# A causal mask moved to GpSimd, four turns moved to TensorE, and new instruction orders in a fused attention and FFN kernel

## The chip, the cores and the metric

The kernel runs on one core of one Trainium2 chip. A core has five engines that run side by side, each through its own list of instructions in order: TensorE (PE in the profile, with its weight loads as PEld), VectorE (DVE), ScalarE (ACT), GpSimd (POOL) and SyncE (SP), which here only issues DMA transfers. An instruction waits until those that it depends on are done, and everything behind it on the same engine waits with it. The metric is the device time of one execution in microseconds.

## The reference

Eight batches of eight heads, 576 positions, 64 channels a head. Attention with a forgetting gate `f`, then a gated FFN with a convolution of three taps over the positions:

```python
scores = scale * np.matmul(q, k.transpose(0, 1, 3, 2))
cum = np.cumsum(np.log(np.clip(f, 0.0001, 1.0)), axis=-1)
decay = cum[:, :, :, None] - cum[:, :, None, :]
scores = np.where(causal, -1000000000.0, scores + decay)
attn = softmax(scores)                       # over the keys
x = np.matmul(attn, v)                       # heads side by side: (8, 576, 512)
h = np.maximum(x @ w_in, 0.0)                # 512 -> 1024
conv_out[s] = cw[0]*h[s-1] + cw[1]*h[s] + cw[2]*h[s+1]
out = (h * sigmoid(conv_out)) @ w_out        # 1024 -> 512
```

The inputs and the output are float32; the kernel computes in 16-bit types with float32 sums.

## The kernel before

The work is cut into 16 half batches `hb` of four heads. Each has two head pairs `i = 2*hb + p`, and two half batches make one batch `b` of the FFN. Every step is a named task of a `Plan`, and the string `ORDER` lists all tasks by hand; `plan.play` calls them in that sequence. As an engine runs its own instructions in order, `ORDER` fixes each engine's list, the SyncE queue included. A suffix `@ACT`, `@DVE` or `@POOL` chooses the engine where a task allows several. Tasks take rooms of small rings: four PSUM tiles `ps`, six `pp` tiles for exponentials, two scratch tiles `pd`, three output tiles `ob`, five `ht`, four `u`.

The tasks, with the lines of their instructions:

- `ld0`, `ld1`, `tp`, `cl`: for half batches 0 and 1, q and k are loaded plainly (L208), turned by TensorE (L215) and copied out of PSUM (L221 on ScalarE, L223 on VectorE). From half batch 2 on, `q{hb}.0` and `q{hb}.1` load and turn q and k in one DMA transpose (L229). Half batches 2 to 7 are clamped by VectorE (L235), and `rw` adds the rows of the decay (L251, L252); from 8 on, `fi` fills these rows by two DMAs instead (L243 from a block of zeros named blank, L245).
- `dca`, `dcl`, `dcs`, `dck`, `ki`: the gate's clip, logarithm, running sum and rows. The gate is loaded twice, into both halves of a tile (L271, L272).
- `sd`, `st`, `so`: scores of the diagonal blocks, the tail and the blocks below the diagonal (L359). `ed`, `et`, `eo`: their exponentials (L400, L379, L417) on ScalarE.
- The causal mask, for the diagonal blocks and the tail only. For half batches in `MASK_PE` TensorE adds a mask into PSUM ahead of the scores (L367), and the exponential goes straight to its 16-bit tile. For the others the exponential goes to a float32 scratch tile, and GpSimd selects from it (`md` at L403, `mt` at L382).
- `v`, `va`: v is loaded (L258) and cast (L266, L268). `pv`: the product with v (L441, L445). `n`: division by the row sum on VectorE (L453, L455).
- Turning x for the FFN: `t` on TensorE (L462, L464) and a copy `tx` (L472); or, for half batches in `XD`, one DMA transpose on SyncE (L467).
- The FFN of batch `b`, in eight blocks `ff`: `f` is the first product (L481), `r` the relu on ScalarE (L491), `c` and `d` the convolution on VectorE (L496, L498), `a` tanh on ScalarE (L501), `g` the gate on VectorE (L505), `o` the second product (L516), `k` copies of the last 64 columns (L510), `e` evacuations (L522, L526) and `s` stores (L532, L537, L540). For the last batch `o7.c.ff` is issued block by block for five chunks `c` of rows.
- `wi`, `wo` load the weights by parts (L551), `wic`, `woc` cast them (L559).

Before, the two choices are:

```python
MASK_PE = (0, 1, 2, 3, 4, 5, 6, 7)
XD = (10, 11, 12, 13, 14, 15)
```

Of the kernel before, what the change touches and what calls it, by code (L numbers as in the profile page):

```python
# [17 lines left out]
ld0 ld0.1.1 ld0.0.0 ld0.0.1 ld0.1.0 tp0.0.0 tp0.0.1 ld1 dca dcl tp0.1.0 tp0.1.1 cl0.0.0@ACT dcs dck ki@POOL ld1.0.0  # L18
cl0.1.0@DVE cl0.1.1@ACT v0.0 cw cl0.0.1@DVE ld1.0.1 tp1.0.0 q2.1 q2.0 v0.2 tp1.0.1 cl1.0.0@ACT cwt cl1.0.1@DVE sd1
tp1.1.0 cl1.1.0@ACT so1.0 eo1.0 v0.3 ed1 tp1.1.1 v0.1 va1.0@POOL cl1.1.1@DVE sd0 so0.0 cl2.0 rw1 so1.1 eo0.0 so0.1  # L20
eo1.1 ed0 v0.4 va1.1@POOL eo0.1 sd2 va0.0@ACT cl2.1 rw2 st0 sd3 so3.0 ed2 wi1 et0 so3.1 eo3.0 so2.1 eo3.1 pv0.0 q3.1
ed3 va0.1@DVE pv0.1 eo2.1 so2.0 eo2.0 wi0 n0.0 st1 et1 cl3.1 wic1@ACT pv1.0 q3.0 pv1.1 wic0@POOL wi3 wic3@POOL q5.0
n1.0 sd4 wi2 wic2@POOL n1.1 t1 q5.1 n0.1 t0 tx0@DVE sd5 tx1@DVE so4.1 ed5 ed4 cl5.0 f0.0 r0.0 st2 eo4.1 f0.1 v1.0 f0.2
r0.1 et2 v1.2 r0.2 so5.0 c0.0 so4.0 eo4.0 cl3.0 d0.0 so5.1 c0.1 d0.1 eo5.1 h0 f0.3 f0.4 rw3 a0.0 r0.3 v1.1 f0.5 cl5.1
f0.6 r0.4 c0.2 g0.0 d0.2 c0.3 v1.3 rw5 eo5.0 a0.1 g0.1 va2.0@DVE wo2 c0.4 sd7 r0.6 c0.6 st3 et3 ed7 sd6 ed6 q4.1 r0.5
so7.1 eo7.1 so6.0 so7.0 eo7.0 eo6.0 d0.4 v1.4 d0.3 d0.6 cl4.1 wo1 va2.1@POOL q4.0 so6.1 st5 eo6.1 pv2.0 sd11 a0.3
va3.0@ACT va3.1@POOL n2.0 c0.5 pv2.1 et5 sd10 wo0 woc0@POOL n2.1 q6.1 t2 g0.3 pv3.0 a0.6 ed11 ed10 pv3.1 q6.0 d0.5
a0.4 tx2@DVE n3.0 a0.2 n3.1 v2.0 f0.7 r0.7 woc2@ACT a0.5 cl4.0 so11.0 woc1@POOL t3 so10.0 so11.1 tx3@DVE v2.3 f1.0
eo11.1 c0.7 d0.7 eo10.0 eo11.0 g0.5 g0.4 g0.6 f1.1 f1.2 r1.0 g0.2 rw4 wo3 f1.3 a0.7 r1.1 so10.1 f1.4 cl6.0 v2.2 v2.4
r1.2 sd8 g0.7 eo10.1 st4 c1.0 r1.4 cl6.1 r1.3 c1.3 d1.3 c1.4 et4 sd9 v2.1 ed8 rw6 so9.0 ed9 d1.0 so9.1 q7.1 f1.5  # L30
woc3@POOL va4.0@DVE o0.0 d1.4 eo9.1 so8.1 eo9.0 q9.0 c1.2 h1 a1.0 q7.0 a1.3 eo8.1 so8.0 v3.0 eo8.0 o0.1 e0.0@ACT c1.1
va5.0@POOL va4.1@ACT sd13 v3.2 g1.0 r1.5 zc v3.1 so13.1 d1.2 eo13.1 k0@DVE f1.6 ed13 pv5.0 g1.3 pv4.0 r1.6 d1.1 n5.0
pv4.1 sd12 n4.0 n4.1 a1.4 va5.1@DVE so12.1 a1.2 g1.2 f1.7 cl7.1 pv5.1 ed12 a1.1 t4 r1.7 c1.7 n5.1 o0.2 v3.3 cl7.0 d1.7
g1.1 tx4@ACT rw7 t5 s0.0 eo12.1 tx5@ACT g1.4 a1.7 c1.6 va7.0@POOL o0.3 so12.0 eo12.0 q9.1 v4.0 so13.0 e0.1@DVE f2.0
v3.4 st6 v4.3 va6.0@POOL sd15 eo13.0 d1.6 et6 f2.1 sd14 c1.5 r2.0 d1.5 c2.0 ed15 r2.1 a1.6 so15.0 g1.7 f2.2 g1.6 d2.0
c2.1 a1.5 ed14 fi9 g1.5 r2.2 f2.3 so14.0 r2.3 f2.4 pv6.0 c2.3 eo14.0 eo15.0 r2.4 n6.0 so14.1 q8.1 so15.1 d2.3 c2.4
o1.0 st9 d2.1 d2.4 eo14.1 eo15.1 st7 h2 a2.0 pv7.0 et7 k1@POOL a2.1 sd19 g2.0 s0.1 et9 a2.3 q8.0 o1.1 va6.1@ACT pv6.1
n7.0 c2.2 q10.0 ed19 e1.0@ACT va7.1@POOL n6.1 fi8 so19.1 eo19.1 f2.5 r2.5 t6 g2.3 f2.6 sd18 tx6@ACT so18.0 r2.6 d2.2
g2.1 c2.5 pv7.1 md19 c2.6 f2.7 q10.1 n7.1 ed18 md18 so19.0 a2.4 g2.4 eo18.0 o1.4 st8 d2.6 eo19.0 d2.5 r2.7 sd16 a2.6
# [67 lines left out]
def kernel(  # L107
# [11 lines left out]
    nc = tc.nc  # L119
# [191 lines left out]
    def decay_log():  # L311
        nc.scalar.activation(fsb, fsb, AF.Ln)
        nc.scalar.preload_act_table(AF.Exp)
# [422 lines left out]
```

## Time and profile before

| what | value |
|---|---|
| median of three runs | 255.22 us (253.63 to 257.57) |
| profiled execution | 254.81 us, of it a span of 253.1 us between first and last instruction |
| granted TensorE clock, mean | 0.985 |
| busy: TensorE, VectorE, ScalarE, GpSimd | 230.6, 215.3, 209.3, 60.2 us |
| DMA | 49.98 MB, mean 197 GB/s |

The page of the profile lists busy time by engine, the span in 40 equal slices (a digit is the busy share in tenths), the chain of work that ended last, and the costliest groups of instructions with their mean duration and the idle time of the engine in front of them, with what ended it. Matmuls are pipelined and their ends are modelled, so a busy TensorE is not one at its peak.

### The profile page before, as it was taken

The page shows a single profiled execution, that of the slowest core. Times are in us where ns is not written, and L with a number is a line of the kernel's source. Part 1 is how long each engine was busy: PE and PEld are TensorE (multiplying, and loading weights), DVE is VectorE, ACT ScalarE, POOL GpSimd, SP SyncE. Part 2 cuts the span into 40 slices and gives each one's busy share as a digit, 9 for nine tenths or more (in the row PEclk, how much of TensorE's full clock was granted, in tenths as well). Part 3 has the DMA queues.
Part 4 walks back from the last instruction along what each step waited for, and adds up shares of the span by engine and source line. Part 5 has one row for each costly group of instructions (what it writes and reads, how often), then busy time and mean ns, then how long its engine had stood idle before and what let it go on. Part 6 is the DMA issues. An engine that isn't in the chain of part 4 may idle for free.

```text
span 253.1 us, 6392 instructions
## 1 busy us (share of the span) xinstructions
PE 230.6 (91%) x2618; PEld 146.2 (58%) x2618; DVE 215.3 (85%) x322; ACT 209.3 (83%) x285; POOL 60.2 (24%) x92
## 2 busy tenths in 40 slices
PE   0799989688999999999999999999959999999992
PEld 0687765357555766766565665665645755644440
DVE  5756064999999999999999989999949999999970
ACT  2746948799899989999899999999957999679661
POOL 8302011101407102221731145402414150000100
PEclk9979999999999999999999999999989999999999
DMA  7993999999999989999999999999998954045046
GB/s 161 326 276 76 218 223 168 233 220 243 223 247 209 218 187 222 237 233 222 194 245 206 242 194 255 213 185 275 230 179 174 198 163 88 7 128 201 6 166 208
DMA packets 121013, 49.98 MB, mean 197 GB/s; under 512 B 111010, under 2 KB 111010, under 8 KB 120984
## 3 DMA queue, kind: packets, MB, share of 16 engines
q1 hardware_dynamic: 120434, 48.41, 88.9%
q0 software_dynamic: 304, 0.73, 0.9%
q10 hardware_dynamic: 246, 0.44, 0.6%
q8 instruction: 20, 0.33, 0.5%
q14 instruction: 9, 0.07, 0.1%
HBM read 21.11 MB, written 10.17 MB: 124 GB/s over the span
## 4 chain that ended last, share of the span: by engine, by line
PE 57%; DVE 15%; DMA 13%; ACT 6%; issue 4%; SPq 2%; POOL 0%; ACTq 0%; DVEq 0%
PE ps L516 21%; PE ps L481 15%; PE ps L359 9%; PE ps L441 6%; DMA qk<-in_q_dram 5%; DVE u L496 4%; DVE u L498 3%; ACT pp L417 3%; DMA qk<-blank 3%; DVE hg L505 2%; DMA qk<-in_k_dram 2%; DMA u<-in_f_dram 2%; PE ps L445 2%; DVE xm L455 1%; PE ps L367 1%
## 5 line engine op out<-in xcount | busy, mean ns | idle before, releaser
L481 PE MATMUL ps<-xt,w_in_f 128*128 128x512 f16 (+1 forms) x512 | 69.3, 286 | 2.1 <-POOL w_in_f L559 1.6
L359 PE MATMUL ps<-qk 128*128 128x64 bf16 (+2 forms) x576 | 63.9, 242 | 4.5 <-DMA qk<-blank 2.6
L417 ACT ACTIVATE pp<-ps 128x1024 f16<-128x1024 f32 x64 | 64.0, 1042 | 2.8 <-PE ps L364 1.9
L516 PE MATMUL ps<-w_out_f,hg 128*128 128x512 f16 x256 | 59.3, 379 | 0.0
L498 DVE SCALAR_TENSOR_TENSOR u<-ht,cwt,u 128x576 f32<-128x576 f16 x64 | 56.2, 895 | 0.7
L496 DVE SCALAR_TENSOR_TENSOR u<-ht,cwt 128x576 f32<-128x576 f16 x64 | 54.0, 853 | 0.8 <-ACT ht L491 0.7
L501 ACT ACTIVATE hg<-u,cw 128x576 f16<-128x576 f32 x64 | 48.8, 788 | 5.5 <-DVE u L498 5.2
L359 PEld LDWEIGHTS <-qk 128*128 128x128 bf16 x576 | 39.8, 99 | 22.9 <-issue 4.6
L481 PEld LDWEIGHTS <-w_in_f 128*128 128x128 f16 x512 | 34.3, 98 | 31.3 <-POOL w_in_f L559 1.9
L505 DVE SCALAR_TENSOR_TENSOR hg<-hg,ht 128x576 f16<-128x576 f16 x64 | 50.2, 810 | 0.5 <-ACT hg L501 0.5
L491 ACT ACTIVATE ht<-ps 128x576 f16<-128x576 f32 x64 | 41.6, 674 | 6.3 <-DVE hg L505 2.6
L516 PEld LDWEIGHTS <-hg 128*128 128x128 f16 x256 | 23.8, 98 | 25.8 <-DVE hg L505 0.8
L403 POOL TENSOR_SCALAR_AFFINE_SELECT pp<-pd 128x1024 f16<-128x1024 f32 x16 | 20.4, 1282 | 55.8 <-ACT pd L400 55.8
L441 PE MATMUL ps<-va,pp 128*128 128x65 f16 x640 | 25.0, 196 | 1.4 <-ACT pp L417 1.2
L455 DVE TENSOR_TENSOR xm<-ps,rc 128x896 f16<-128x896 f32 (+1 forms) x32 | 24.2, 758 | 1.1
L441 PEld LDWEIGHTS <-pp 128*128 128x128 f16 x640 | 23.0, 99 | 3.7 <-ACT pp L417 1.1
L400 ACT ACTIVATE pd<-ps 128x1024 f32<-128x1024 f32 x16 | 16.4, 1041 | 5.0 <-PE ps L359 4.2
L400 ACT ACTIVATE pp<-ps 128x1024 f16<-128x1024 f32 x16 | 16.1, 1040 | 4.1 <-PE ps L359 4.1
L510 POOL COPY tl<-hg 128x512 f16<-128x512 f16 (+1 forms) x9 | 5.9, 669 | 45.6 <-DVE hg L505 45.6
L453 DVE RECIPROCAL rc<-ps 128x14 f32<-128x14 f32 (+1 forms) x32 | 6.6, 206 | 11.5 <-PE ps L441 7.7
L367 PE MATMUL ps<-mask,ident 128*128 128x512 bf16 (+1 forms) x40 | 14.7, 370 | 0.7 <-ACT pp L417 0.6
L266 POOL CAST va<-vf 128x1024 f16<-128x1024 f32 x7 | 8.5, 1226 | 25.9 <-PE ps L359 11.6
(91 smaller groups left out, 202.8 us busy)
## 6 DMA issues: line engine op xcount, KB each, us to landing
vf<-in_v_dram SPq DMA_DIRECT2D x32, 256.0 KB, 4.3
out_dram<-ob SPq DMA_DIRECT2D x14, 512.0 KB, 2.8
qk<-blank SPq DMA_DIRECT2D x8, 540.0 KB
ob<-in_moe_w_in_dram SPq DMA_DIRECT2D x4, 512.0 KB
ob<-in_moe_w_out_dram SPq DMA_DIRECT2D x4, 512.0 KB, 4.6
vf<-in_v_dram SPq DMA_DIRECT2D x8, 128.0 KB, 2.9
out_dram<-ob SPq DMA_DIRECT2D x4, 256.0 KB
out_dram<-ob SPq DMA_DIRECT2D x7, 128.0 KB, 2.8
```

Source lines behind the costliest of these rows:

```text
L359: nc.tensor.matmul(o, tk[:, h * S + k0:h * S + k0 + 128], tq[:, h * S + q0:h * S + q0 + n], start=first, stop=last and not by_matmul(hb, h))
L400: nc.scalar.activation(o, ps_of(f"sd{i}").rearrange("p (s c) -> p s c", s=2), AF.Exp, scale=SCALE)
L417: nc.scalar.activation(pair(i)[:, s, 512:1536], ps_of(f"so{i}.{s}"), AF.Exp, scale=SCALE)
L441: nc.tensor.matmul(ps[:, c:c + D + 1], block(hb, h, m, n), va[:, h, m, 0:D + 1], start=(m == 0), stop=(m == n))
L455: nc.vector.tensor_tensor(x.rearrange("p (j h d) -> p j h d", j=a, d=D), got[:, :, :, 0:D], r.unsqueeze(3).broadcast_to((128, a, g, D)), o ...
L481: nc.tensor.matmul(ps[:, c:c + n], w_in_f16[:, cc, 128 * ff:128 * (ff + 1)], xt[:, cc // 2, x:x + n], start=(cc == 0), stop=(cc == NCC - 1))
L491: nc.scalar.activation(ht_of(b, ff)[:, 1:1 + S], ps_of(f"f{b}.{ff}")[:, 0:S], AF.Relu, scale=0.5)
L496: nc.vector.scalar_tensor_tensor(u, ht[:, 0:S], cwt[:, ff, 0:1], ht[:, 1:1 + S], op0=ALU.mult, op1=ALU.add)
L498: nc.vector.scalar_tensor_tensor(u, ht[:, 2:2 + S], cwt[:, ff, 1:2], u, op0=ALU.mult, op1=ALU.add)
L501: nc.scalar.activation(hg_of(b, ff), u_t[slot[f"c{b}.{ff}", "u"]], AF.Tanh, scale=cw[:, ff, 1:2])
L505: nc.vector.scalar_tensor_tensor(hv, hv, 1.0, ht_of(b, ff)[:, 1:1 + S], op0=ALU.add, op1=ALU.mult)
L516: nc.tensor.matmul(ps[:, 512 * (c % 2):512 * (c % 2 + 1)], w, w_out_f16[:, ff, :], start=(ff == 0), stop=(ff == NFF - 1))
```

## The change

1. Half batches 4 to 7 leave `MASK_PE`: their mask is applied by GpSimd (`md8` to `md15`, `mt4` to `mt7`), as it already is for 8 to 15.
2. Half batches 10 to 13 leave `XD`: their x is turned on TensorE and copied; 14 and 15 stay with the DMA.
3. The second copy of the gate is loaded from SyncE's queue instead of ScalarE's.
4. The load of the Exp table becomes a task `tb` of its own, which the order places.
5. The relu may run on VectorE; seven do (`r0.0 r0.6 r1.0 r2.6 r3.0 r5.1 r5.4`). The weight casts may too; one does (`woc2`).
6. Chunk 1 of the last batch is evacuated and stored in two halves of 256 columns, on ScalarE and VectorE, from SyncE's and ScalarE's queues. It is now the chunk that ends last; before it was chunk 3.
7. The whole order is new, with other engine choices. Copies of x on VectorE go from 7 to 8 and on ScalarE from 3 to 6; of the short v casts (`va{hb}.1`) VectorE has six instead of two; of the output evacuations it has two and a half chunk instead of four; GpSimd loses one cast each of v, w_in and w_out and two copies `k`.

```diff
-    MASK_PE = (0, 1, 2, 3, 4, 5, 6, 7)
-    XD = (10, 11, 12, 13, 14, 15)
+    MASK_PE = (0, 1, 2, 3)
+    XD = (14, 15)
...
-    nc.scalar.dma_start(fsb[BH:128], f.rearrange("b h s -> (b h) s"))
+    nc.sync.dma_start(fsb[BH:128], f.rearrange("b h s -> (b h) s"))
...
         nc.scalar.activation(fsb, fsb, AF.Ln)
-        nc.scalar.preload_act_table(AF.Exp)
...
-    def relu(b, ff):
-        nc.scalar.activation(ht_of(b, ff)[:, 1:1 + S], ps_of(f"f{b}.{ff}")[:, 0:S], AF.Relu, scale=0.5)
+    def relu(b, ff, e):
+        o, i = ht_of(b, ff)[:, 1:1 + S], ps_of(f"f{b}.{ff}")[:, 0:S]
+        if e == "ACT":
+            nc.scalar.activation(o, i, AF.Relu, scale=0.5)
+        else:
+            nc.vector.tensor_scalar(o, i, 0.5, 0.0, op0=ALU.mult, op1=ALU.max)
...
+    def evac_half(b, c, x):
+        o = ob_t[slot[f"e{b}.{c & ~1}", "ob"]][:, c % 2, 256 * x:256 * (x + 1)]
+        i = ps_of(f"o{b}.{c & ~1}.0")[:, 512 * (c % 2) + 256 * x:512 * (c % 2) + 256 * (x + 1)]
+        (nc.vector.tensor_copy if x else nc.scalar.copy)(o, i)
+
+    def store_half(b, c, x):
+        r = b * S + 128 * c
+        (nc.scalar if x else nc.sync).dma_start(outf[r:r + 128, 256 * x:256 * (x + 1)],
+                                                ob_t[slot[f"e{b}.{c & ~1}", "ob"]][:, c % 2, 256 * x:256 * (x + 1)])
...
+    add("tb", "ACT", [], lambda: nc.scalar.preload_act_table(AF.Exp), behind=["dcl"])
```

The order at three places, the engine lists written out: `SP` is SyncE's queue, `PE` TensorE's list.

```
start, SP before: ld0.1.1 ld0.0.0 ld0.0.1 ld0.1.0 ld1.0.0 v0.0 ld1.0.1 q2.1 q2.0 v0.2 v0.3 v0.1 rw1 v0.4 rw2
                  wi1 q3.1 wi0 q3.0 wi3 q5.0 wi2 q5.1 v1.0 v1.2 rw3 v1.1 v1.3 rw5
start, SP after:  (gate) ld0.0.0 ld0.0.1 ld0.1.0 ld0.1.1 ld1.0.0 ld1.0.1 v0.0 v0.4 q2.1 q2.0 v0.3 v0.2 rw1 wi0
                  v0.1 q3.0 wi1 rw2 q3.1 wi3 q5.0 wi2 rw3 q5.1 v1.0 v1.3 v1.4 v1.2 v1.1 rw5
late, SP before:  q13.0 v6.0 v6.3 fi13 q14.1 v6.2 v6.1 tx10 s3.0 tx11 v6.4 s1.1 q14.0 v7.0 v7.1 fi14 s3.2 q15.0
                  q15.1 v7.3 v7.2 fi15 tx12 tx13 s3.1 s4.0 v7.4 tx14 s5.2 tx15
late, SP after:   q13.1 s0.0 v6.0 fi13 v6.1 s1.1 s3.0 q15.1 v6.2 v6.3 q14.1 q14.0 s2.1 v6.4 fi14 v7.0 v7.1 v7.3
                  v7.2 s3.2 q15.0 v7.4 fi15 s4.1 s3.1 tx14 tx15
late, PE before, from fi14 to the scores of half batch 14: so27.1 f5.4 f5.5 sd28
late, PE after:                                            so24.1 o4.0 o4.1 f5.5 st14
end, PE before, from the first use of the last gate: o7.0.7 o7.2.6 o7.2.7 o7.1.7, o7.4.1 to o7.4.7, o7.3.1 to o7.3.7
end, PE after: o7.0.7 o7.4.2 o7.1.1 o7.2.6 o7.2.7 o7.4.3 o7.3.5 to o7.3.7, o7.4.4 to o7.4.7, o7.1.2 to o7.1.7
```

More of the change, by code (lines that the diff above doesn't have):

```diff
@@ L17 @@
 ORDER = """
[L18 to L27, printed above, removed]
@@ L694 @@
             for c in range(NKB):
+                if c == 1:
+                    for x in range(2):
+                        add(f"e{b}.{c}.{x}", ("ACT", "DVE")[x], [f"o{b}.{c}.{NFF - 1}"], lambda b=b, c=c, x=x: evac_half(b, c, x),
+                            behind=[f"e{b}.{c - 1}"])
+                        add(f"s{b}.{c}.{x}", ("SP", "ACT")[x], [f"e{b}.{c}.{x}"], lambda b=b, c=c, x=x: store_half(b, c, x))
+                    continue
                 add(f"e{b}.{c}", "ACT/DVE", [f"o{b}.{c}.{NFF - 1}"], lambda e, b=b, c=c: evac_chunk(b, c, e),
```

106 lines of the change are left out of this document (60 added, 46 removed).

## The prediction

> **What bounds the kernel now.** I read the busy shares first, then the span in slices.
>
> ```profile
> PE 230.6 (91%) x2618; PEld 146.2 (58%) x2618; DVE 215.3 (85%) x322; ACT 209.3 (83%) x285; POOL 60.2 (24%) x92
> ...
> PE   0799989688999999999999999999959999999992
> ...
> DVE  5756064999999999999999989999949999999970
> ...
> DMA  7993999999999989999999999999998954045046
> ```
>
> Three engines are close together, and only POOL is free. The averages hide the stages, so the next view is the busy time by stretch. I cut it at the first late arrival of q (42.5 us), where the pipeline is full (68), and around the hole that the slices show near 180. The columns are the length, then busy time and count of PE, PEld, DVE, ACT and POOL, then PE's granted clock, the DMA share and GB/s.
>
> ```profile
> 0.00:42.50 42.50, 33.22 (x425) 25.57 (x426) 21.66 (x47) 26.04 (x29) 10.82 (x38) 0.96 0.94 206
> 42.50:68.00 25.50, 20.83 (x281) 13.97 (x280) 24.69 (x35) 22.73 (x32) 5.14 (x5) 1.00 1.09 229
> 68.00:148.00 80.00, 79.27 (x949) 50.50 (x948) 77.21 (x111) 76.16 (x105) 21.42 (x24) 1.00 1.08 222
> 148.00:175.00 27.00, 26.50 (x313) 16.70 (x311) 26.37 (x37) 25.67 (x37) 8.98 (x9) 1.00 1.09 225
> 175.00:188.00 13.00, 10.36 (x118) 6.30 (x116) 10.02 (x14) 10.21 (x16) 3.83 (x4) 0.97 1.10 219
> 188.00:249.00 61.00, 60.40 (x548) 33.17 (x546) 55.33 (x81) 48.49 (x73) 10.02 (x12) 0.98 0.50 135
> ```
>
> From 42.5 us on VectorE idles 0.8, 2.8, 0.6 and 3.0 us in the first four of the later stretches; of the 5.7 us in the last one most lies after its last gate at 243.5 (row below). From 68 on TensorE idles 0.7, 0.5, 2.6 and 0.6 us. So **two engines are full at once**, and ScalarE trails by 4 us in 80. Freeing TensorE pays only as far as VectorE can follow. The last window has the DMA share at half: after 188 no transfer holds anything up.
>
> VectorE's work is three lines for each of the 64 blocks of the FFN. Here are their groups (busy, mean ns) and their spreads (min/median/max ns, first and last start):
>
> ```profile
> L498 DVE SCALAR_TENSOR_TENSOR u<-ht,cwt,u 128x576 f32<-128x576 f16 x64 | 56.2, 895 | 0.7
> L496 DVE SCALAR_TENSOR_TENSOR u<-ht,cwt 128x576 f32<-128x576 f16 x64 | 54.0, 853 | 0.8 <-ACT ht L491 0.7
> L505 DVE SCALAR_TENSOR_TENSOR hg<-hg,ht 128x576 f16<-128x576 f16 x64 | 50.2, 810 | 0.5 <-ACT hg L501 0.5
> ...
> L498 DVE SCALAR_TENSOR_TENSOR u<-ht,cwt,u x64: 804/810/1698, 44.8 to 241.4; 128x576 f32<-128x576 f16 x64
> L496 DVE SCALAR_TENSOR_TENSOR u<-ht,cwt x64: 803/810/1635, 43.3 to 238.6; 128x576 f32<-128x576 f16 x64
> L505 DVE SCALAR_TENSOR_TENSOR hg<-hg,ht x64: 742/748/1650, 50.0 to 243.5; 128x576 f16<-128x576 f16 x64
> ```
>
> The means lie 85, 43 and 62 ns above the medians: 190 ns x 64 = 12.2 us of VectorE go into a few long ones. One of them, with the POOL instruction beside it:
>
> ```profile
> 125.22 1.54 POOL L403 TENSOR_SCALAR_AFFINE_SELECT pp<-pd 128x1024 f16<-128x1024 f32 x1
> ...
> 125.74 1.64 DVE L496 SCALAR_TENSOR_TENSOR u<-ht,cwt 128x576 f32<-128x576 f16 x1
> ...
> L403 POOL TENSOR_SCALAR_AFFINE_SELECT pp<-pd x16: 1092/1136/1645, 110.4 to 204.1; 128x1024 f16<-128x1024 f32 x16
> ```
>
> The select ends at 126.76, and the conv that began at 125.74 ends 0.62 us later. A conv that overlaps a select waits for it, here for 1.64 - 0.81 = 0.83 us. The change adds such selects.
>
> **The masks of half batches 4 to 7.** They take 16 matmuls of 512 columns and 4 of 256 from TensorE. The price of a wide matmul is read from a block of eight in the chain, and of a transpose likewise:
>
> ```profile
> 89.60 0.55 PE ps L462 x8
> 90.20 1.73 PE ps L516 x8
> ```
>
> 1.73 / 8 = 0.216, so 16 x 0.216 + 4 x 0.108 = **3.9 us off TensorE**, between about 68 and 100 us. Added are 8 selects of about 1.14 us and 4 small ones on POOL, which has room (21.4 busy of 80). Each pv of these half batches now waits for exp and then select, about 1.2 us more. Behind it in TensorE's queue stand ffn1 and ffn2 blocks of 1 to 1.7 us; the new order puts several of them between the last exp and the pv for half batches 4, 5 and 7, and for 6 a v cast that pv needs anyway, so I charge nothing; uncovered it would be 4 x 1.2 = 4.8 us. The second scratch room of pd also makes the exp of pair 9 wait for the select of pair 11, with woc0 and the exps of pair 10 ahead of it as cover.
>
> What the selects do to VectorE: about 50 POOL casts, copies and selects run after 40 us and share the 12.2 us, 0.24 us each. The change has 12 selects more, and 5 casts and copies fewer: 7 x 0.24 = **+1.7 us on VectorE**. The ends are 0 (all miss) and 12 x 0.83 = 10.0 (all hit, the small ones priced as the large). I take the mean of this trace, since the 16 present selects show both.
>
> The Trainium skill (SBUF — State Buffer, section "SBUF: two separate sides") says that VectorE with two SBUF inputs and a GpSimd instruction that reads SBUF contend for one shared port pair, an "exclusive lock, not a bandwidth split": the later one waits for the whole instruction. The pair at 125 us agrees. By that rule every select that starts first costs what is left of it, which speaks for the upper end.
>
> **Turns of half batches 10 to 13.** Four DMA transposes leave SyncE's queue:
>
> ```profile
> 167.07 3.04 SPq L467 DMA_TRANSPOSE xt<-xm  x1
> 170.82 1.66 SPq L467 DMA_TRANSPOSE xt<-xm  x1
> 195.65 5.12 SPq L467 DMA_TRANSPOSE xt<-xm  x2
> ```
>
> That is 9.8 us of queue time, with their waits for the norms. TensorE gets 36 transposes: 36 x 0.55 / 8 = **+2.5 us**. Together with the masks TensorE loses 1.4 us. The four copies out of PSUM go two to ScalarE, two to VectorE.
>
> **VectorE's list by the new order.** Counting the engine suffixes, after its first q wait:
>
> ```profile
> L526 DVE COPY ob<-ps 128x512 f32<-128x512 f32 x1 | 0.7, 692 | 0.8 <-PE ps L516 0.8
> L522 DVE COPY ob<-ps 128x1024 f32<-128x1024 f32 x2 | 2.4, 1219 | 0.3 <-PE ps L516 0.3
> L472 DVE COPY xt<-ps 128x1152 f16<-128x1152 f16 x7 | 5.1, 751 | 1.0 <-PE ps L464 1.0
> L266 DVE CAST va<-vf 128x1024 f16<-128x1024 f32 x5 | 3.5, 690 | 0.6 <-issue 0.6
> L268 DVE CAST va<-vf 64x256 f16<-64x256 f32 x2 | 0.6, 278 | 1.3 <-DMA vf<-in_v_dram 1.3
> ```
>
> Seven relus come over. No VectorE relu is in this trace; between 0.69 us for 512 columns and 1.22 for 1024, 576 columns give 0.76. One falls into the startup wait: 6 x 0.76 = 4.6. One turn copy more: 0.75. Three short v casts more: 0.8. One w_out cast: 0.7, priced as the v cast of that shape. Two evacuations of 1024 columns (2.4) leave, two of 512 stay in number, one half chunk comes (0.4): -2.0. Tails +0.3. One clamp is already done in the startup: -0.9. The sum is 4.3. Back to back the next one starts before a row's duration is over: the select's row at 125 above shows a conv of 0.81 done in 0.62 once released. I take a tenth off, **+3.9 us**, between 2 and 5.
>
> ScalarE loses the relus and gains a w_in cast, three turn copies and two evacuations, about +2 us; its gap of 4 in 80 holds that.
>
> **The start.**
>
> ```profile
> 1.39 0.61 ACTq L272 DMA_DIRECT2D u<-in_f_dram  x1
> ...
> 21.06 0.72 SPq L252 DMA_DIRECT2D qk<-image  x1
> ...
> 24.61 4.05 SPq L229 DMA_TRANSPOSE qk<-in_k_dram  x1
> ...
> 34.60 5.82 SPq L229 DMA_TRANSPOSE qk<-in_q_dram  x1
> ...
> 42.51 0.88 DVE L235 TENSOR_SCALAR qk<-qk,lim 128x2304 uint16<-128x2304 uint16 x1 [3.40 <-DMA qk<-in_q_dram]
> ```
>
> The second gate copy on SyncE starts 0.6 us earlier there and pushes every load behind it back by as much: nothing, either way. The Exp table load moves behind the first two turned tiles, and scores begin with pair 0, so the first exps come sooner. The rows of half batch 1 wait for all four of its turned tiles, the last of them on VectorE; scores of pair 0 stand ahead of two of these turns, so I let the rows go 0.7 us sooner than at 21.06. From there to the transpose of q5 at 34.60 the new order has the same rows, loads and transposes in another sequence, without the waits of half a microsecond between them. So q5, and the wait to 42.5, move by **-1.2 us**, ends 0 and -3.
>
> **The hole at 180.**
>
> ```profile
> 173.98 5.88 DMA qk<-in_q_dram
> ...
> 179.87 6.46 DMA qk<-blank
> ...
> 186.43 1.04 PE ps L359 x12
> ...
> 188.65 0.18 DVE L453 RECIPROCAL rc<-ps 128x4 f32<-128x4 f32 x1 [3.35 <-PE ps L445]
> ```
>
> The last q of half batch 14 stands behind two x transposes and a store, its fill behind it, and the scores wait. In the new order both x transposes are gone (4.7 us), but one transpose of half batch 15, of about 4, stands ahead instead. With 1.2 us from the start, and two ffn2 blocks (2 x 1.73) between the fill and its first scores where one more ffn1 block stood, I take the hole as closed: **-3.35 us** on VectorE, ends 0 and -3.35. What is late next is VectorE itself.
>
> The other waits of VectorE from 42.5 to 175 (4.2 us) are short ones, some for TensorE, which is freer there: I take half, **-2.1**, ends 0 and -4.2.
>
> **The end.** 19 small matmuls instead of 18 stand from the first that needs the last gate: **+0.2 us** where VectorE decides.
>
> ```profile
> 248.43 0.58 ACT L526 COPY ob<-ps 128x512 f32<-128x512 f32 x1 [0.88 <-PE ps L516]
> 249.04 0.34 SPq L532 DMA_DIRECT2D out_dram<-ob  x1
> ```
>
> Halves on two engines and two queues save half of the copy and some of the landing: **-0.5**, ends 0 and -1.
>
> **The sum**, on VectorE's path: 1.7 + 3.9 - 1.2 - 3.35 - 2.1 + 0.2 - 0.5 = -1.35, a span of 251.75 after 253.1. The profiled execution took 254.81, the median of the runs is 255.22, 2.1 above its span: **253.9 us**.
>
> **Rivals.**
> 1. TensorE decides: VectorE's added 3.9 us find room, as its busy figure counts latencies that overlap. Then -1.4 for TensorE's work, -1.2 start, -2.6 hole, -0.5 end, and of its 4.7 us idle between 42.5 and 68 about 1: 246.4, or **248.5 us**. For it: the chain of waits lies on TensorE from 188 to the end. Against: VectorE has no room before 175. Chance 0.23.
> 2. The selects hit: each starts first and holds the conv behind it, 10.0 instead of 1.7 us, 260.05 or **262.2 us**. It decides from 0.7 us a select (8.2 us). For it: the pair at 125. Against: a quarter of a microsecond is the mean here. Chance 0.10. The lock that the Trainium skill describes (SBUF — State Buffer), taken by every select, would come out here.
> 3. The change doesn't close the hole: the transpose of half batch 15 takes the place of the two x transposes. +3.35: **257.2 us**. Chance 0.15.
>
> My forecast has 0.52. About 2% is what a measurement of this kernel can tell from no change, so 250.1 to 260.3 is "same": the forecast and rival 3, 0.67; faster 0.23; slower 0.10. The range reaches from below rival 1 to above rival 3: 247.5 to 259.0; left out are rival 2 and the lowest part of rival 1.
>
> **What would show it.** 20 mask matmuls on L367 instead of 40 and two x transposes in SyncE's queue; VectorE's three lines with means above 913, 870 and 820 ns if selects hit more than I charge, and VectorE's relus at about 0.76; the wait for q5 ending near 41.3; no wait of TensorE for blank; VectorE full to its last gate with TensorE now idling more than 1 us in 80. TensorE full and VectorE with gaps would be rival 1. I am wrong on the whole if the new order, which I only counted and did not follow instruction by instruction, opens or closes waits elsewhere.

## The result and the profile after: no change that the medians show

In the comparison made for the result the changed kernel took 256.37 us (median of 20 runs, 254.27 to 258.63) and the kernel before 256.35 us (20 runs, 252.62 to 259.49). The ratio is 1.0123, 95% interval 1.0089 to 1.0156. That ratio leaves disturbed runs out, and since the kernel before spreads further both ways it keeps mostly its low ones; the profile before is itself of a run counted as disturbed, at a granted clock of 0.985 where the profile after has 0.996. The changed kernel run again in another comparison gave 1.0025 (0.9987 to 1.0062). So it is not faster; it lies between no change and 1.2% slower. The forecast was 1.3 us faster, 253.9 after 255.22, which was the median of only three runs.

The page of the changed kernel, first the busy times and the slices (columns as before):

```profile
span 252.8 us, 6429 instructions
...
PE 228.4 (90%) x2634; PEld 145.3 (57%) x2634; DVE 216.5 (86%) x334; ACT 211.5 (84%) x283; POOL 67.8 (27%) x99
...
PE   0999778887898999999999999799999999999992
...
DVE  5454086999997999999999999989899999999961
```

The hole near 180 is gone from both slice rows. But TensorE now shows more sevens and eights between slices 4 and 12 (counted from 0), and a seven in slice 25. The same stretches as before:

```profile
42.50:68.00 25.50, 20.78 (x291) 14.41 (x290) 24.85 (x38) 24.88 (x34) 5.41 (x5) 1.00 1.10 229
68.00:148.00 80.00, 78.36 (x935) 49.83 (x934) 77.45 (x112) 76.27 (x104) 27.76 (x29) 1.00 1.05 202
148.00:175.00 27.00, 25.35 (x312) 16.10 (x311) 25.40 (x38) 23.69 (x35) 6.68 (x7) 1.00 1.08 246
175.00:188.00 13.00, 12.81 (x84) 6.43 (x80) 12.15 (x17) 12.67 (x16) 5.61 (x6) 1.00 1.05 216
188.00:249.00 61.00, 59.27 (x602) 33.76 (x602) 55.17 (x84) 47.34 (x71) 10.84 (x14) 1.00 0.42 124
```

From 175 to 188 VectorE idles 0.85 us instead of 2.98. From 148 to 175 it idles 1.60 instead of 0.63, and TensorE 1.65 instead of 0.50. Over the four stretches up to 188 VectorE's idle time falls from 7.2 to 5.65 us. Its three FFN lines:

```profile
L502 DVE SCALAR_TENSOR_TENSOR u<-ht,cwt 128x576 f32<-128x576 f16 x64 | 54.1, 853 | 1.9 <-ACT ht L495 1.7
L504 DVE SCALAR_TENSOR_TENSOR u<-ht,cwt,u 128x576 f32<-128x576 f16 x64 | 54.1, 859 | 0.8
L511 DVE SCALAR_TENSOR_TENSOR hg<-hg,ht 128x576 f16<-128x576 f16 x64 | 47.9, 773 | 1.6 <-ACT hg L507 1.5
```

and their spreads:

```profile
L502 DVE SCALAR_TENSOR_TENSOR u<-ht,cwt x64: 801/810/1646, 43.2 to 239.1; 128x576 f32<-128x576 f16 x64
L504 DVE SCALAR_TENSOR_TENSOR u<-ht,cwt,u x64: 798/812/1769, 44.7 to 239.9; 128x576 f32<-128x576 f16 x64
L511 DVE SCALAR_TENSOR_TENSOR hg<-hg,ht x64: 743/750/1604, 48.6 to 242.7; 128x576 f16<-128x576 f16 x64
```

The medians are those of before. The means lie 43, 47 and 23 ns above them, 113 ns x 64 = 7.2 us (7.5 in one expectation below) where it was 12.2. This excess is contention with GpSimd. Laid over GpSimd's timeline, the instructions of these lines that meet no GpSimd instruction lose 0.1 us or less in all, in either trace. Those beside a select lose 7.4 us before and 6.2 after, those beside a cast 4.6 and 1.1. So there are 12 selects more, and less contention on these three lines. But some of it has moved to another line, the clamps of q and k. Here are the rows of VectorE and then of GpSimd:

```profile
88.28 3.37 DVE L238 TENSOR_SCALAR qk<-qk,lim 128x2304 uint16<-128x2304 uint16 x2
...
88.23 1.03 POOL L331 DMA_DIRECT2D image<-zero  x2
89.25 0.72 POOL L332 DMA_DIRECT2D blank<-zero  x1
89.97 1.05 POOL L269 CAST va<-vf 128x1024 f16<-128x1024 f32 x1
90.96 1.64 POOL L405 TENSOR_SCALAR_AFFINE_SELECT pp<-pd 128x1024 f16<-128x1024 f32 x1
```

The two clamps take 1.59 and 1.85 us, the first beside GpSimd's DMA instructions and the second mostly beside its cast and select, where the median clamp takes 0.87. That is 1.7 us lost, and in the kernel before no clamp behind 42.5 us lost any. From 42.5 us on the contention on VectorE is thus 8.9 us after 12.2.

The start and the end: VectorE's longest wait up to 43 us (in total, times, longest), and then rows of the timelines.

```profile
DVE qk L238 <- DMA qk<-in_q_dram: 9.6, 1, 9.6
```

```profile
42.08 0.87 DVE L238 TENSOR_SCALAR qk<-qk,lim 128x2304 uint16<-128x2304 uint16 x1
...
242.75 0.75 DVE L511 SCALAR_TENSOR_TENSOR hg<-hg,ht 128x576 f16<-128x576 f16 x1
...
245.83 0.58 ACT L532 COPY ob<-ps 128x512 f32<-128x512 f32 x1 [2.94 <-PE ps L522]
...
246.45 0.69 DVE L532 COPY ob<-ps 128x512 f32<-128x512 f32 x1 [1.22 <-ACT ob L532]
...
248.00 0.37 ACT L537 COPY ob<-ps 128x256 f32<-128x256 f32 x1 [0.67 <-PE ps L522]
...
248.40 0.42 DVE L537 COPY ob<-ps 128x256 f32<-128x256 f32 x1 [1.26 <-ACT ob L537]
248.86 0.38 ACTq L541 DMA_DIRECT2D out_dram<-ob  x1
```

VectorE's clamp of q5 comes 0.43 us sooner than before (42.08 for 42.51). The wait of 9.6 us is for q3, whose clamp the new order puts ahead of q5's. From the clamp to the end of the last gate (242.75 + 0.75 = 243.50) lie 201.4 us; before, with the last gate at 243.5 and its end at 244.25, 201.7. From there to the end of the span lie 9.3 us; before, 8.85. The three differences, -0.4, -0.3 and +0.4, make up the -0.3 us between the spans.

### The profile page after: what moved, and what is told of

Read it like the earlier page. It is cut to its first block, busy times and chain, and to the rows that moved or that the text cites. A ratio compares the mean times of both kernels' runs of the same rounds, so it can differ in the third digit from the quotient of the medians.

```text
span 252.8 us, 6429 instructions
## 1 busy us (share of the span) xinstructions
PE 228.4 (90%) x2634; PEld 145.3 (57%) x2634; DVE 216.5 (86%) x334; ACT 211.5 (84%) x283; POOL 67.8 (27%) x99
## 4 chain that ended last, share of the span: by engine, by line
PE 46%; DMA 14%; SPq 13%; DVE 11%; ACT 10%; issue 5%; ACTq 0%; DVEq 0%
PE ps L522 16%; PE ps L483 11%; SPq L232 9%; PE ps L361 8%; DMA vf<-in_v_dram 5%; PE ps L443 4%; ACT pp L419 3%; DMA qk<-blank 3%; SPq L261 2%; DMA qk<-in_q_dram 2%; DVE xm L457 2%; DMA out_dram<-ob 2%; DMA hg<-in_q_dram 2%; DVE hg L511 2%; ACT pd L402 2%
## 5 line engine op out<-in xcount | busy, mean ns | idle before, releaser
L419 ACT ACTIVATE pp<-ps 128x1024 f16<-128x1024 f32 x64 | 64.8, 1038 | 7.0 <-PE ps L361 4.3
L361 PE MATMUL ps<-qk 128*128 128x128 bf16 (+2 forms) x576 | 62.2, 240 | 4.7 <-ACT pp L419 0.9
L502 DVE SCALAR_TENSOR_TENSOR u<-ht,cwt 128x576 f32<-128x576 f16 x64 | 54.1, 853 | 1.9 <-ACT ht L495 1.7
L511 DVE SCALAR_TENSOR_TENSOR hg<-hg,ht 128x576 f16<-128x576 f16 x64 | 47.9, 773 | 1.6 <-ACT hg L507 1.5
L405 POOL TENSOR_SCALAR_AFFINE_SELECT pp<-pd 128x1024 f16<-128x1024 f32 x24 | 30.9, 1294 | 62.7 <-ACT pd L402 62.7
L495 ACT ACTIVATE ht<-ps 128x576 f16<-128x576 f32 x57 | 37.1, 662 | 4.9 <-PE ps L483 4.1
L402 ACT ACTIVATE pd<-ps 128x1024 f32<-128x1024 f32 x24 | 24.6, 1033 | 1.0 <-PE ps L361 0.9
L238 DVE TENSOR_SCALAR qk<-qk,lim 128x2304 uint16<-128x2304 uint16 x12 | 12.1, 1013 | 9.6 <-DMA qk<-in_q_dram 9.6
L528 ACT COPY ob<-ps 128x1024 f32<-128x1024 f32 (+1 forms) x17 | 16.0, 940 | 4.5 <-PE ps L522 2.4
L516 POOL COPY tl<-hg 128x64 f16<-128x64 f16 (+1 forms) x7 | 5.2, 764 | 37.0 <-DVE hg L511 37.0
L384 POOL TENSOR_SCALAR_AFFINE_SELECT pt<-p 128x256 f16<-128x256 f32 x12 | 7.9, 660 | 23.2 <-ACT p L381 23.2
```

Of the source, the lines that this page charges most:

```text
L361: nc.tensor.matmul(o, tk[:, h * S + k0:h * S + k0 + 128], tq[:, h * S + q0:h * S + q0 + n], start=first, stop=last and not by_matmul(hb, h))
L402: nc.scalar.activation(o, ps_of(f"sd{i}").rearrange("p (s c) -> p s c", s=2), AF.Exp, scale=SCALE)
L405: nc.gpsimd.affine_select(pair(i)[:, :, 0:512].rearrange("p s (m j) -> p s m j", j=128), pd_t[slot[f"ed{i}", "pd"]].rearrange("p s (m j) - ...
L419: nc.scalar.activation(pair(i)[:, s, 512:1536], ps_of(f"so{i}.{s}"), AF.Exp, scale=SCALE)
L495: nc.scalar.activation(o, i, AF.Relu, scale=0.5)
L502: nc.vector.scalar_tensor_tensor(u, ht[:, 0:S], cwt[:, ff, 0:1], ht[:, 1:1 + S], op0=ALU.mult, op1=ALU.add)
```

## The experiments

The theories that the expectations name: **L**, loads on SyncE's queue pin the times; **V**, VectorE decides; **T**, TensorE decides; **B**, the three engines and SyncE's queue are balanced, so that what is saved on one is taken up by the others; **O**, the parts gain and the new order loses. The expectations that name **H**, **W**, **X** and **N** say what these are. Each time is a median, with that of the kernel before in the same comparison behind the stroke, and the ratio to it with its 95% interval.

### Cutting one resource at a time, in the changed kernel

Each of these leaves a part of the computation out, only to free one resource.

```diff
# s1_dma: the DMA transposes of q of half batches 8 to 15 carry two heads of four
-    lambda hb=hb, side=side: load_qk(hb, 0, 4, side)
+    lambda hb=hb, side=side: load_qk(hb, 0, 2 if hb >= 8 and side == 0 else 4, side)
# s2_dve: the second conv of the odd ff does half of its columns
-    scalar_tensor_tensor(u, ht[:, 2:2 + S], ...)
+    n = S // 2 if ff % 2 else S
+    scalar_tensor_tensor(u[:, 0:n], ht[:, 2:2 + n], ...)
# s3_pe: the second product of ff 1, 3 and 5 does 256 columns of 512
-    matmul(ps[:, 512 * (c % 2):512 * (c % 2 + 1)], w, w_out_f16[:, ff, :], ...)
+    n = 256 if ff in (1, 3, 5) else 512
+    matmul(ps[:, 512 * (c % 2):512 * (c % 2) + n], w, w_out_f16[:, ff, 0:n], ...)
# s4_act: from batch 2 on, tanh of three in four ff does half of its columns
+    n = S // 2 if b > 1 and (ff % 2 or ff % 4 == 2) else S
# c1_dve_pe_act = s2 + s3 + s4;  c2_all = c1 + s1;  c0_after: the changed kernel, no edit
```

> The changed kernel, but the q transposes of half batches 8 to 15 load only two of four heads (the others stay as the ring left them), some 16 us of SyncE's queue less. Theory L (the loads on SyncE's queue pin both kernels: the chain holds transposes and the fill of half batch 14 until 188 us): 8 to 15 us faster than before, the fill of half batch 14 lands before 178 us. Theory V (VectorE's list decides): at most 3 us, for the hole near 180. Theory T (TensorE decides): about 3 us too.

> The changed kernel, but the second conv instruction of each odd block works on half of its columns, 32 x 0.3 = 9.6 us of VectorE less. Theory V: 7 to 10 us faster than before. Theory L and theory T: within 3 us of before.

> The changed kernel, but the second product of blocks 1, 3 and 5 adds into half of the columns, 108 matmuls x 0.107 = 11.5 us of TensorE less. Theory T: 8 to 11 us faster than before. Theory V: within 2 us. Theory L: 2 to 4 us, from the stretch after 190 us alone, where no load is left.

> The changed kernel, but tanh of blocks 1, 2, 3, 5, 6 and 7 of batches 2 to 7 works on half of its columns (the rest of the tile is left from earlier), 36 x 0.27 = 9.7 us of ScalarE less. Theories L, V and T: within 2 us of before. A gain of 5 us or more would make ScalarE the bound.

> The changed kernel as it is, beside the others of this call. All theories: a median within 0.5% of before's median, as in the 20 runs of each (256.37 and 256.35).

> The changed kernel with the cuts of VectorE (9.6 us), TensorE (11.5 us) and ScalarE (9.7 us) made together; cut alone they moved the median by -0.9%, -0.1% and +0.2% of before. The same halves of columns are left out as there. Theory B (three engines in balance through queues in fixed order, each holds the time when another is cut): 7 to 10 us faster than before. Theory L (the loads on SyncE's queue pin the kernel whatever the engines do): at most 3 us faster.

> The three cuts and the shorter q transposes of half batches 8 to 15 (16 us of SyncE's queue) together. Theory B: 1 to 3 us below the kernel with the three engine cuts. Theory L: 8 us or more below it.

| kernel | cut | us / before | ratio |
|---|---|---|---|
| s1_dma | SyncE's queue, 16 us | 255.42 / 255.27 | 1.0015 (0.9978 to 1.0051) |
| s2_dve | VectorE, 9.6 us | 252.88 / 255.27 | 0.9876 (0.9802 to 0.9950) |
| s3_pe | TensorE, 11.5 us | 254.94 / 255.27 | 0.9984 (0.9940 to 1.0027) |
| s4_act | ScalarE, 9.7 us | 255.90 / 255.27 | 1.0045 (0.9993 to 1.0097) |
| c0_after | none | 256.53 / 256.04 | 1.0025 (0.9987 to 1.0062) |
| c1_dve_pe_act | three engines | 249.85 / 256.04 | 0.9743 (0.9679 to 0.9806) |
| c2_all | all four | 248.78 / 256.04 | 0.9655 (0.9569 to 0.9741) |

The cuts in the table are estimates from the rows' durations. In the traces the busy time fell by less: 7.5 us on VectorE (216.5 to 209.0), 7.3 on TensorE (228.4 to 221.1), 6.6 on ScalarE (211.5 to 204.9); the eight shortened q transposes fell from 30.2 to 16.7 us. Such a cut gives 2.4 us on VectorE and nothing measurable on the others. The cut on SyncE's queue gives nothing, although the fill of half batch 14 starts at 175.86 us there instead of 180.78. All three engines together give 6.7 us against c0_after, the changed kernel in the same comparison, and the cut on the queue another 1.1, which is not clear of the noise.

L and T fall by these numbers. V falls as it stood, with 2.4 us of its 7 to 10, though VectorE is the only engine that answers alone. B comes nearest: the engines answer together where they don't alone. Its 7 to 10 us against the kernel before were narrowly missed (6.2), and that SyncE's queue is a fourth balanced resource is not shown. What s3_pe leaves in the trace:

```profile
68.00:148.00 80.00, 73.81 (x918) 48.63 (x915) 77.68 (x111) 76.11 (x103) 28.92 (x29) 1.00 1.04 205
```

TensorE has 6 us of room in 80, and VectorE (77.68) and ScalarE (76.11) carry on at the same pace.

### Undoing one part, in the changed kernel

```diff
# p1_mask_pe: the twelve tasks md8 to md15 and mt4 to mt7 leave the order too
-    MASK_PE = (0, 1, 2, 3)
+    MASK_PE = (0, 1, 2, 3, 4, 5, 6, 7)
# p2_xd: t10 to t13 leave the order, tx10 to tx13 become DMA transposes where they stand
-    XD = (14, 15)
+    XD = (10, 11, 12, 13, 14, 15)
# p3_q15_late, in the order
-    s3.0 q15.1 ... q14.1 ... q14.0 ... fi14
+    s3.0 ... q14.1 ... q14.0 ... fi14 q15.1
# p4_relu_act, in the order, and so with the other six
-    r0.0@DVE
+    r0.0@ACT
```

> The changed kernel with the masks of half batches 4 to 7 back on TensorE (12 selects less on GpSimd, 20 mask matmuls more, nothing else moved). Prediction's step (selects cost VectorE 1.7 us net, masks 3.9 us of TensorE): V says 0 to 2 us faster than the changed kernel, T says 3 to 4 us slower, L says no change.

> The changed kernel with x of half batches 10 to 13 turned by DMA again, at the places where their copies stand. L says 3 to 6 us slower (four more transposes in a full queue, each waiting for its norm); V says 1 us faster (two copies of 0.75 us off VectorE); T says 2 us faster (36 transposes off TensorE).

> The changed kernel with one transpose moved: k of half batch 15, which took 5.9 us of SyncE's queue at 164 us ahead of half batch 14's two transposes, goes behind the fill of half batch 14. Rival 3 of the prediction (the hole stays because this transpose takes the place of the x transposes): the fill of half batch 14 goes at 175 instead of 180.8, and the time falls by 2 to 4 us. If VectorE or TensorE decides: no change.

> The changed kernel with the seven relus on VectorE back on ScalarE (7 x 0.76 us off VectorE, 7 x 0.66 us onto ScalarE). V says 3 to 4 us faster; L and T say no change; if ScalarE is the tighter one, 2 to 3 us slower.

| kernel | us / before | ratio |
|---|---|---|
| p1_mask_pe | 256.30 / 257.27 | 1.0009 (0.9963 to 1.0055) |
| p2_xd | 268.70 / 257.27 | 1.0471 (1.0402 to 1.0540) |
| p3_q15_late | 257.14 / 257.27 | 1.0023 (0.9975 to 1.0071) |
| p4_relu_act | 258.36 / 257.27 | 1.0109 (1.0061 to 1.0158) |

Within the new order the masks are worth nothing in time, and with four half batches' masks back on TensorE the contention on the three lines stays as it is:

```profile
L501 DVE SCALAR_TENSOR_TENSOR u<-ht,cwt 128x576 f32<-128x576 f16 x64 | 54.7, 863 | 2.3 <-ACT ht L494 2.1
L503 DVE SCALAR_TENSOR_TENSOR u<-ht,cwt,u 128x576 f32<-128x576 f16 x64 | 53.9, 856 | 0.8
L510 DVE SCALAR_TENSOR_TENSOR hg<-hg,ht 128x576 f16<-128x576 f16 x64 | 47.8, 773 | 0.6 <-ACT hg L506 0.5
```

116 ns over the medians (812, 813, 751) is 7.4 us with 16 wide selects; the two profiles of the changed kernel (the one above and c0_after) have 7.2 and 8.0 with 24. The clamps lose 0.7 us here (all beside the DMA instructions), and 1.7 and 2.6 there. So in the new order the 12 selects cost VectorE 0.8 to 2.5 us. The turns on TensorE are worth about 12 us in this order, more than any theory said, as TensorE waits for those of the DMA: in p2_xd the waits of TensorE from 150 to 230 us and its busy time in the old hole are

```profile
PE ps L482 <- DMA xt<-xm: 9.0, 3, 5.5
```

```profile
175.00:188.00 13.00, 7.93 (x49) 4.36 (x49) 7.58 (x10) 5.75 (x9) 2.31 (x2) 0.74 1.09 238
```

p3_q15_late puts the load of half batch 14 ahead of the transpose that I had called its obstacle: its fill then starts at 179.85 instead of 180.78 (182.70 in c0_after), not at 175, and the time stays. p4_relu_act makes VectorE wait 8.3 us for relus (`DVE u L502 <- ACT ht L495: 8.3, 8, 1.8`); against p1 and p3 of the same comparison (1.001 and 1.002) the relus on VectorE are worth about 0.9%, 1 to 2 us. V, which expected a gain of 3 to 4 us, misses its sign. The loss is near what was expected if ScalarE were the tighter engine, yet ScalarE's cut alone had given nothing.

### The two moves alone, in the old order

```diff
# b1_mask: the kernel before; each new md and mt stands right behind its ed and et in the order
-    MASK_PE = (0, 1, 2, 3, 4, 5, 6, 7)
+    MASK_PE = (0, 1, 2, 3)
# b2_xd: the kernel before; t10 to t13 stand a few tasks behind their norms, their copies a few behind them,
# two on ScalarE and two on VectorE
-    XD = (10, 11, 12, 13, 14, 15)
+    XD = (14, 15)
# b3_mask_xd = b1 + b2
# b4_mask_split (b1, the eight added wide selects) and a1_split (the changed kernel, all 24)
-    affine_select(pair(i)[:, :, 0:512], pd, pattern=[[0, 2], [0, 4], [1, 128]], ...)
+    for s in range(2):
+        affine_select(pair(i)[:, s, 0:512], pd[:, s, :], pattern=[[0, 4], [1, 128]], ...)
```

> The kernel before in its own order, with only the masks of half batches 4 to 7 on GpSimd (each select right behind its exp) and x of 10 to 13 turned on TensorE (each turn three places behind its norm, its copy six places later). Prediction's sum without a new order (masks +1.7 us on VectorE for 12 more selects at 0.24 us each is 2.9, hole -3.35, two copies +1.5): within 2 us of before. Theory B: no change either, as TensorE's 1.4 us are lost in the other two. Theory O (the parts gain and the new order gives it back): 3 to 6 us faster than before.

> The kernel before, with its own order, and only the mask of half batches 4 to 7 moved to GpSimd, each select right behind its exponential. Theory H (VectorE is held by the selects): most of the 8.3 us that the two edits cost together are the mask's, +5 to +7 us, 261 to 263 us; the excess of VectorE's three FFN lines over their medians rises from 12.2 us to 17 or more, and 68 to 148 us holds fewer matmuls. Theory W (the product with v waits for the exponential and then the select): also +4 to +6 us, but the excess stays near 12 and TensorE shows new waits for POOL. Theory X (the turns are the cost): +0 to +2 us, 256 to 258.

> The kernel before, with its own order, and only x of half batches 10 to 13 turned on TensorE and copied, two copies on ScalarE and two on VectorE. Theories H and W: small, +0 to +3 us, 256 to 259; the prediction's sum for this edit alone is +2.5 us of TensorE and +0.75 of VectorE less the hole at 180 us. Theory X: +5 us or more, 261 or above, lost after 160 us where the turns stand.

> As the kernel before with the mask of half batches 4 to 7 on GpSimd (the old order), but each of these eight wide selects is cut in two instructions of 512 columns. Theory H: a conv that comes second waits for a select half as long, so a third to half of that kernel's loss goes: 258 to 260 us, excess of VectorE between 13 and 16 us. Theory W: the two halves take a little longer than the whole, so the product with v waits longer: no better than the uncut one, 261 to 264.

> The changed kernel, with all 24 wide selects cut in two instructions of 512 columns. Theory H: of its 7.5 us of excess some 4.5 us lie beside selects; half of that goes, but only part of it reaches the end as the engines are balanced: -0.5 to -1.5 us, 255 to 256. Theory W: +0.5 to +1.5 us, 257 to 258.

The last column is the excess of VectorE's three FFN lines over their medians, 12.2 us in the kernel before.

| kernel | us / before | ratio | over the medians |
|---|---|---|---|
| b3_mask_xd | 264.33 / 256.04 | 1.0291 (1.0227 to 1.0356) | 18.8 us |
| b1_mask | 258.25 / 256.45 | 1.0077 (1.0024 to 1.0131) | 17.1 us |
| b2_xd | 260.12 / 256.45 | 1.0139 (1.0074 to 1.0205) | 12.4 us |
| b4_mask_split | 259.72 / 256.45 | 1.0115 (1.0041 to 1.0189) | 17.7 us |
| a1_split | 255.77 / 256.45 | 0.9984 (0.9940 to 1.0028) | 9.4 us |

In the old order, at the places that I gave them, each move costs by itself, 1.8 and 3.7 us, and both together 8.3, so O falls too: the parts lose there, and in the new order they don't. The prediction's own sum for the two moves, within 2 us, and B, which had no change, miss as well. The new order with neither move was not run. The masks lose as the second rival said. From the timelines of GpSimd and VectorE of b1_mask:

```profile
76.67 2.97 POOL L403 TENSOR_SCALAR_AFFINE_SELECT pp<-pd 128x1024 f16<-128x1024 f32 x2
...
77.16 1.53 DVE L498 SCALAR_TENSOR_TENSOR u<-ht,cwt,u 128x576 f32<-128x576 f16 x1
78.61 1.64 DVE L496 SCALAR_TENSOR_TENSOR u<-ht,cwt 128x576 f32<-128x576 f16 x1
```

the spread of its selects, and two of its stretches:

```profile
L403 POOL TENSOR_SCALAR_AFFINE_SELECT pp<-pd x24: 1089/1422/2537, 66.6 to 207.1; 128x1024 f16<-128x1024 f32 x24
```

```profile
68.00:148.00 80.00, 72.47 (x839) 45.41 (x839) 78.68 (x101) 71.40 (x98) 36.96 (x35) 1.00 1.02 203
175.00:188.00 13.00, 13.00 (x131) 7.67 (x130) 12.65 (x17) 12.98 (x21) 4.75 (x5) 1.00 1.17 253
```

Two selects and two convs alternate, and each waits for the one before it: convs of 0.81 take 1.53 and 1.64, and the median select goes from 1.14 to 1.42 us. In 68 to 148 VectorE is as busy as ever and gets 101 instructions done instead of 111; TensorE falls from 79.3 to 72.5, only 3.9 of which are the masks that left. This is the exclusive lock that the Trainium skill describes (SBUF — State Buffer, section "SBUF: two separate sides"). The trace agrees. Yet only 1.8 us reach the end: the hole at 180 is filled in b1_mask (13.00 of 13), so part of the delay seems to be taken out of the wait for half batch 14. Theory H had +5 to +7 us: right on the mechanism, too high on its size. Of W the waits show one thing: TensorE waits 2.1 us for a cast of w_out that stands behind the selects on GpSimd (`PE ps L516 <- POOL w_out_f L559: 2.1, 1, 2.1`), and none for a select.

Cutting selects in two, which should have halved each hold, took no contention away (17.7 us against 17.1; 9.4 against 7.2 and 8.0 in the changed kernel). More of the convs and gates meet a select: 44 instead of 40 in the old order, 35 instead of 30 in the new. The two times, 259.72 and 255.77 us, lie in H's ranges, but not by H's way, and the ratios do not differ beyond the noise from those of the uncut kernels, b1_mask and c0_after. H's remedy falls.

The turns alone lose 3.7 us, though SyncE's queue is freed: VectorE waits 3.2 us for turns (`DVE xt L472 <- PE ps L464: 3.2, 2, 2.2`), since I had put each copy soon behind its turn. That is above the 0 to 3 of H and W and under the 5 of X.

### One new wait of the new order taken away

In both profiles of the changed kernel ScalarE waits for a store, and TensorE behind it. The changed kernel, engines ScalarE, TensorE and SyncE's queue:

```profile
157.80 0.58 SPq L553 DMA_DIRECT2D out_dram<-ob  x1
...
162.61 1.01 ACT L528 COPY ob<-ps 128x1024 f32<-128x1024 f32 x1 [2.02 <-DMA out_dram<-ob]
...
163.67 0.61 PE L464 MATMUL ps<-ident,xm 128*128 128x128 f16 x8 [1.32 <-ACT ob L528]
```

The store of batch 0 stands behind the transpose of q13. The evacuation needs its output tile, and the turn of half batch 10 needs the evacuation's PSUM room: a wait that the kernel before didn't have, and part of the 1.2 us that TensorE loses between 148 and 175.

```diff
# a2_s0_first, in the order
-    c3.7 q13.1 mt10 d3.7 ... so22.1 s0.0 h4
+    c3.7 s0.0 q13.1 mt10 d3.7 ... so22.1 h4
# a3_ob4: output tiles
-    NOB = 3
+    NOB = 4
```

> The changed kernel with one store of batch 0 (s0.0) put ahead of the second transpose of half batch 13 on SyncE's queue instead of behind it, so that it is issued some 4 us sooner. Theory N (this one new wait gives the hole's gain back): ScalarE's wait for the store of 2.0 to 2.8 us and TensorE's of 1.3 to 1.8 us behind it both vanish, and 1 to 2 us of the end with them: 254.5 to 255.5. Theory B (four balanced resources, each short wait is taken up by the next): the waits vanish but the end moves by 0.8 us at most: 255.7 to 256.7.

> The changed kernel with four output tiles instead of three, so that an evacuation takes a room that no store holds; the order is the same. Both theories expect no wait of ScalarE for a store. Theory N: 1 to 2 us gained, 254.5 to 255.5, the same as with the earlier store. Theory B: 0 to 0.8 us gained, 255.7 to 256.7.

a2_s0_first: 257.59 / 255.81, 1.0155 (1.0056 to 1.0253). a3_ob4: 255.52 / 255.81, 1.0104 (1.0019 to 1.0188). Both waits are gone from both traces, and the ratios show no gain; the changed kernel itself, which had 1.0123 and 1.0025 elsewhere, was not in this comparison. In a2_s0_first the next waits of TensorE from 148 on are

```profile
PE ps L483 <- DVE xm L457: 1.3, 1, 1.3
PE ps L361 <- DMA qk<-blank: 0.5, 1, 0.5
```

where the first is as long as the one removed. The gain of 1 to 2 us that N named isn't seen. Neither theory's range holds a2_s0_first's 257.59, which lies above both, and a3_ob4's 255.52 lies between the two; that the next wait takes up the one removed, as B has it, rests on the waits of a2_s0_first. No version that does all the work was faster than both kernels beyond the noise.

## Why the prediction was wrong, point by point

- **The step that failed: the two terms for waits, each booked at its full length.** The hole (-3.35) and half of the other waits (-2.1) were to give 5.45 us. The prediction asked "what is late next" of the hole and answered "VectorE itself". In the trace the hole went (VectorE idles 0.85 us for 2.98), but VectorE's other waits up to 175 us grew by 0.6, so that 1.6 us of idle time were saved, not 5.45. TensorE saved 2.5 us of its idle time in the hole and lost most of it again before: from 42.5 to 188 us it idles 8.2 us after 8.5. VectorE's busy time had meanwhile grown by 1.4 us, so that its last gate ends only 0.3 us sooner after q5's clamp. The cuts show why a single saving pays so little: three engines are so close that some 7 us off one are worth 0 to 2.4, and only the three together reach the end.
- **The selects**: +1.7 us forecast, -3.3 measured (8.9 for 12.2, the clamps counted; in c0_after 10.6, so -1.6). A mean per GpSimd instruction was carried to an order in which the instructions meet other neighbours; most of the fall on the three lines lies beside casts (4.6 to 1.1). With the order kept, the 12 selects cost VectorE 4.9 us of contention (b1_mask, 17.1 for 12.2, 0.41 each), inside the bounds 0 to 10. With the new order the same 12 cost 0.8 to 2.5 (p1_mask_pe). The second rival's mechanism is real, but neither its condition nor its price came about.
- **VectorE's list**: its busy time from 42.5 to 249 rose by 195.0 - 193.6 = 1.4 us; with 3.3 us less contention the list itself grew by about 4.7. That is above the +3.9 that was forecast, inside its ends of 2 and 5, and near the 4.3 of the count before a tenth was taken off. The relus are as priced:

```profile
L497 DVE TENSOR_SCALAR ht<-ps x7: 751/755/762, 41.4 to 183.0; 128x576 f16<-128x576 f32 x7
```

  0.755 us for 0.76.
- **The hole**, -3.35. It closed by -2.1, but not in the way that was forecast:

```profile
164.07 5.86 SPq L232 DMA_TRANSPOSE qk<-in_k_dram  x1
...
171.22 4.08 SPq L232 DMA_TRANSPOSE qk<-in_k_dram  x1
175.35 3.36 SPq L232 DMA_TRANSPOSE qk<-in_q_dram  x1
...
180.78 0.87 SPq L246 DMA_DIRECT2D qk<-blank  x1
...
188.21 1.18 PE L361 MATMUL ps<-qk 128*128 128x64 bf16 x20 [0.40 <-DMA qk<-blank]
```

  The transpose of half batch 15 took 5.86 us of the queue where two x transposes had taken 4.7, and the fill starts 0.9 us later than before (179.87). The third rival had this right, and its 257.2 us lies nearer to the measured 256.37 than the forecast, but by luck, as the hole closed all the same. What fills it is TensorE's list: from 175 to 188 it has 12.81 us of other work before these scores, which then wait 0.40 us for blank.
- **The other waits**, -2.1. From 42.5 to 175 VectorE's idle time went from 4.23 to 4.80, +0.6: wrong in sign.
- **The start**, -1.2: -0.43 by the clamp of q5, inside its ends of 0 and -3, but nearer to nothing.
- **The end**, +0.2 and -0.5. The halves of the last chunk do not run side by side: VectorE's starts at 248.40, 0.03 us after ScalarE's ends (248.00 + 0.37), and the trace names ScalarE's copy as its releaser. The -0.5 was not there, and the tail became 0.4 us longer. The Trainium skill (PSUM — Partial Sum Buffer, section "PSUM bank collisions raise a hardware error") says that the compiler adds a dependency between any two instructions on different engines that touch the same PSUM bank in the same quadrant of partitions, reads too. The row agrees with that, and I had not looked there. Whether it is the bank or the shared tile that orders them was not separated. The copies of chunks 2 and 3, which read different 512-column halves of one PSUM tile, follow each other in the same way (ScalarE's ends at 245.83 + 0.58 = 246.41, VectorE's starts at 246.45), so the order is not confined to parts of one chunk.
- **Rival 1**, TensorE decides: refuted by s3_pe. **What would show it**: 20 mask matmuls and two x transposes came as said; "VectorE full and TensorE idling more than 1 us in 80" came too (1.6), without the gain that was to follow. TensorE's wait for blank did not go, and the wait for q5 ended at 42.08, not near 41.3.
- **The sum**: the spans differ by -0.3 us where -1.35 was forecast. That they lie only 1.05 us apart is luck: contention came out 5.0 us lower than its term, and the hole (1.2), the other waits (2.7), the list, the start and the end (about 0.8 each) together some 6 us higher.
- What the prediction put last as its weakness, an order that was counted and not followed, opened the wait at 162 us; but taking that wait away gained nothing.

## What to carry to other kernels

Before a saved wait is booked as time, ask whether the engines beside it could run on without it; in this kernel, whose order has been fitted until three engines stand at 83 to 91%, a cut on one of them was worth a third of itself or nothing, and only cuts on several at once reached the end. The cost of contention depends on the order, not on the instruction alone: the same 12 selects cost 4.9 us of VectorE in one order and 0.8 to 2.5 in the other, so a moved GpSimd instruction is priced by its neighbours on VectorE. Two edits that each lose can break even with a new order around them, so such a change has to be judged as one piece.

## What had not been expected of the hardware

- Selects and two-input convs that alternate slow each other both ways: convs of 0.81 take up to 1.69 us, selects with a median of 1.14 take 1.42 in the median and 2.54 at the longest (b1_mask). Halving the selects does not lessen it. Clamps of q and k are held too: one of 0.87 us takes 1.85 beside a cast and a select, and 3.44 in c0_after.
- Two executions of the same program differ by more than the terms argued about. The changed kernel's two profiles have spans of 252.8 and 256.3 us, and much of the difference lies between 148 and 175. There the second (c0_after) has

```profile
148.00:175.00 27.00, 24.60 (x287) 14.94 (x284) 22.88 (x35) 21.57 (x31) 6.48 (x7) 0.94 1.07 237
```

  VectorE at 22.88 instead of 25.40 and a granted TensorE clock of 0.94 instead of 1.00. Which of the two came first, the idle VectorE or the lower clock, was not separated. Differences of a microsecond between two traces, as used above, are to be read with that in mind.
